# Local attention cut into 32-query pieces: six groups of 192 queries in place of ten, and strided value products in four array tiles

## The chip, the cores and the metric

The kernel runs on one core of a Trainium2 chip. The metric is device time in microseconds (us), the median of three runs of the whole program. The names of the engines are those of the profile: PE is TensorE, DVE is VectorE, ACT is ScalarE, POOL is GpSimd, SP is SyncE, whose queue issues all DMA transfers here.

## The reference

Attention over 2 sequences, 8 heads, 576 positions, 64 numbers per head; then two feed-forward parts on the 1152 tokens that come out. The change touches only the attention.

```python
rel = pos[:, None] - pos[None, :]
mask_local   = (rel >= 0) & (rel < 32)                          # heads 0 to 3
mask_strided = (rel >= 0) & (pos[None, :] % 32 == pos[:, None] % 32)   # heads 4 to 7
scores = np.where(masks, scale * q @ k.T, -1e9)
attn = softmax(scores)            # maximum taken off, sum + 1e-9 below
x = (attn @ v)                    # to [1152 tokens, 512]
h = np.maximum(x @ w_in, 0.0);  x = (h * h) @ w_out             # 512 -> 2048 -> 512
out = sum over e of p[:, e] * (np.maximum(x @ w1[e], 0.0) @ w2[e])     # 4 experts, 512 -> 1024 -> 512
```

A query of a local head sees 32 keys: its own and the 31 before it. A query of a strided head sees at most 18: the positions with its own remainder by 32.

## The kernel before

**Stages.** The tokens are three blocks of 384. The first feed-forward part takes block 0 (steps of one 128-wide slice of the 2048 hidden columns each), then block 1, then a part in which blocks are taken in pairs with fewer products, then the experts. Each large product is three matmuls of one pass (lines 788 to 790, of `mm3`; lines 1328 to 1330 for the experts), 384 or 512 columns wide. Block 0 needs the attention of the first 384 positions of sequence 0, so three strided and three local groups of that sequence come first ("startup"); the other groups are put between the steps of blocks 0 and 1 ("second", "third").

**One attention group** (`attend`). Loads of k, q and v by SP; scores on PE into a PSUM bank; a mask, either added on PE by a matmul with the identity (`ON_PE`, lines 426 and 497) or by DVE (line 554); the maximum on DVE (561); then either one exponent per unit on ACT with the sum beside it (566), or, where `whole` is set, a subtraction on DVE (571), one exponent on ACT (572) and a sum on DVE (573); reciprocal (574, 575); a product with it on POOL or DVE (576); transposes on PE (435 strided, 506 local); a copy to `pt` on ACT or DVE (545, 547); value products on PE (447 strided, 516 local); and the results as a rounded part (587, 589) and a rest (593) into `x`. The operands of scores and values are 4-byte floats; each of these matmuls stands in the trace as two records.

**Local groups.** A group is 128 queries (two groups: 64) of four heads. A unit is 64 queries of two heads (2 x 64 = 128 rows) on 64 + 32 = 96 keys. Scores: two matmuls of 64 x 64 weights and 96 columns per unit, one in rows 0 to 63 of the array with results in partitions 0 to 63, the other in rows and partitions 64 to 127. Each unit has one transpose and two value matmuls with 96 rows, 64 columns of weights and 64 columns of data. There are 18 units in a sequence.

**Strided groups.** 4 x 3, 4 x 3 or 4 x 2 remainders a group, three groups in a sequence, eight units. The value matmuls stand in two 64 x 64 parts of the array: rows 0 to 63 to partitions 0 to 63, and 64 to 127 to 64 to 127.

**Order.** `Plan.run` is a list scheduler that runs when the kernel is built. Each task has costs in ns by engine, a rank, what it comes after and the buffers that it takes; the model's order becomes the order on each engine's queue. While PE has nothing ready early on, it gives PE matmuls of no use on the tile `idle` (line 1477, `filler`), until the first product of step 0. The ranks come from constants (`FIRST` for the startup scores, `LKQ` and `LV` for their loads, `EARLY`, `LW`, `CONV`, `FETCH` for weights).

Of the kernel before, what the change touches and what calls it, by code (L numbers as in the profile page):

```python
# [33 lines left out]
CB = P + 2 * WIN + N3 + N2  # L34
NEG = -8.0e9
# [33 lines left out]
class Plan:  # L69
# [9 lines left out]
    SAME, CROSS, DMA = 100, 200, 2200  # L79
# [14 lines left out]
    def add(self, engines, emit, after=(), rank=0, take=(), free=(), adds=(), behind=None, quiet=False, tenses=(), relaxes=(), port=False):  # L94
        t = Plan.Task()
        t.engines = dict(engines)
# [7 lines left out]
    def run(self):  # L104
        import heapq

        waits, then = {}, {}
# [6 lines left out]
        events, count, done, now, fill = [], 0, 0, 0, True  # L114
# [11 lines left out]
        while done < len(self.tasks):  # L126
# [4 lines left out]
            while events and events[0][0] == now:  # L131
# [6 lines left out]
                elif what == "end":  # L138
                    t = x
                    done += 1  # L140
                    for env, key in t.free:
                        ring, tile_ = env["_" + key]
                        self.rings[ring].append(tile_)
                    for ring, tiles in t.adds:
                        self.rings[ring] += tiles
                    for y in then.get(t, ()):
                        waits[y] -= 1
                        lag = 0 if y.behind is t or t.ran == "pe" and "pe" in y.engines else self.DMA if t.ran == "dma" else self.SAME if t.ran in y.engines else self.CROSS
# [3 lines left out]
            for e in ready:  # L152
                while idle[e] and ready[e]:
                    held, got = [], None
                    while ready[e]:
# [4 lines left out]
                        if not (t.quiet and e in self.tense or (t.port or e == "pool") and now < self.shared) and all(any(self.rings[r] for r in rings) for _, _, rings in t.take):  # L160
                            got = t
                            break
# [5 lines left out]
                    for env, key, rings in got.take:  # L168
                        r = next(r for r in rings if self.rings[r])
                        tile_ = self.rings[r].pop(0)  # L170
                        env[key], env["_" + key] = tile_, (r, tile_)
# [6 lines left out]
                    got.end = now + int(got.engines[e] * slow)  # L178
                    order.append((now, len(order), got.emit, e))
# [18 lines left out]
def tile_attention_mlp_experts(ctx: ExitStack, tc: tile.TileContext, a, out):  # L198
# [25 lines left out]
    AHEAD = 10013  # L224
    END2 = 24614
    END3 = 330
    CONV = 22941
    R_LOW, R_HI = 5016, 616
    CONV1 = 31773
    CONV2 = -8455  # L230
    FETCH = 252
    WITH2 = 817
    PE_SLICE = 1914
    SQ = (0, 23, 0)
    R_MASK = -916
    ON_PE = (1, 0, 1, 0, 0, 0, 0, 0, 0, 0)
    FILL = 0
    R_MAX = -6105
    R_EXP = -6564
    R_NORM = 9634  # L240
    R_T = 1235
    R_V = 6312
    R_X = 13702
    R_LO = -53571
    R_OUT = 2681
    FIRST = (-22394, 16695, 607, 23035, 8563, 1593)
    WHOLE = (1, 1, 1, 0, 0, 0)
# [61 lines left out]
    def mm_r(n):  # L309
        return int(n / 2.4) + 13  # L310
# [1256 lines left out]
```

## Time and profile before

| what | us |
|---|---|
| median of 3 runs | 615.62 (615.57 to 615.78) |
| span of the profiled execution | 614.7 |
| PE busy in the span | 608.4 (99%) |
| DVE busy | 452.9 (74%) |
| ACT busy | 302.4 (49%) |
| POOL busy | 125.4 (20%) |
| granted TensorE clock, mean | 0.999 |

The profile gives the span of its one execution, from the first instruction to the last, and no other time of it; the runs' median is 0.92 us above that span. Shares are of the span. The times of matmuls overlap, because they are pipelined: what one of them takes from PE is read from the distance between starts, not from its duration.

### The profile page before, as it was taken

The numbers are of one execution on the slowest core, as the hardware profiler recorded it, in microseconds if no ns is written. First come the engines' busy times: TensorE is split into PE (matmuls) and PEld (weight loads), VectorE is DVE, ScalarE is ACT, GpSimd is POOL, SyncE is SP. The second block draws the span as 40 slices with busy tenths as digits, with TensorE's granted clock in tenths as the row PEclk, the third lists the DMA queues.
The fourth block names the chain that finished last, engine by engine and source line by source line (L and its number), as shares of the span: only waits on it lengthen the run. The fifth ranks groups of instructions, "written<-read, shape, count | busy, mean of one in ns | idle before, by whom it ended". The sixth has DMA issues, their size and how long they took to land.

```text
span 614.7 us, 10054 instructions
## 1 busy us (share of the span) xinstructions
PE 608.4 (99%) x3737; PEld 558.4 (91%) x3737; DVE 452.9 (74%) x900; ACT 302.4 (49%) x705; POOL 125.4 (20%) x150
## 2 busy tenths in 40 slices
PE   8999999999999999999999999999999999999997
PEld 5898999999999999998898989898998989898996
DVE  5997958774797984977666675858866776987654
ACT  3676875656464653665244534344344534344330
POOL 2421202310010101032031231312141322224000
PEclk9999999999999999999999999999999999999999
DMA  8987332131213100020110202020201203020012
GB/s 262 315 262 204 110 110 92 34 108 66 102 50 89 36 0 18 1 86 18 38 49 20 84 18 86 18 86 17 71 16 36 70 17 86 18 86 1 1 52 103
DMA packets 37441, 45.14 MB, mean 73 GB/s; under 512 B 4688, under 2 KB 26640, under 8 KB 37392
## 3 DMA queue, kind: packets, MB, share of 16 engines
q1 hardware_dynamic: 37392, 44.50, 23.7%
q8 instruction: 29, 0.48, 0.3%
q14 instruction: 20, 0.16, 0.1%
HBM read 42.13 MB, written 2.36 MB: 72 GB/s over the span
## 4 chain that ended last, share of the span: by engine, by line
PE 97%; DMA 1%; ACT 0%; DVE 0%; SPq 0%; issue 0%; POOL 0%; ACTq 0%
PE bh L788 12%; PE bh L790 12%; PE bh L789 12%; PE by L1329 11%; PE by L1328 11%; PE by L1330 11%; PE by L788 5%; PE by L790 5%; PE by L789 5%; PE ba L788 4%; PE ba L790 4%; PE ba L789 3%; PE ba L516 1%; PE ba L502 1%; DMA q<-in_ql_dram 1%; DMA k<-in_ks_dram 1%
## 5 line engine op out<-in xcount | busy, mean ns | idle before, releaser
L1281 DVE SCALAR_TENSOR_TENSOR acc<-by,pe,acc 128x512 f32<-128x512 f32 (+1 forms) x109 | 79.3, 743 | 24.2 <-PE by L1330 23.9
L788 PE MATMUL bh<-x,w 128*128 128x384 f32 x234 | 80.4, 344 | 0.0
L790 PE MATMUL bh<-x,w 128*128 128x384 f32 x234 | 78.4, 335 | 0.0
L789 PE MATMUL bh<-x,w 128*128 128x384 f32 x234 | 78.4, 335 | 0.0
L1226 POOL TENSOR_TENSOR sf<-raw,raw 128x256 f32<-128x256 f32 x40 | 32.1, 812 | 185.8 <-DMA raw<-in_w_dram 95.9
L1237 ACT ACTIVATE w<-sf 128x256 fp32r<-128x256 f32 x110 | 42.0, 406 | 35.8 <-POOL sf L1226 35.8
L1329 PE MATMUL by<-o,h 128*128 128x512 f32 (+1 forms) x134 | 52.3, 390 | 0.0
L1328 PE MATMUL by<-o,h 128*128 128x512 f32 (+1 forms) x134 | 52.0, 388 | 0.0
L788 PE MATMUL by<-h,w 128*128 128x384 f32 x152 | 51.8, 341 | 0.0
L1330 PE MATMUL by<-o,h 128*128 128x512 f32 (+1 forms) x134 | 51.7, 386 | 0.0
L790 PE MATMUL by<-h,w 128*128 128x384 f32 x152 | 50.8, 334 | 0.0
L789 PE MATMUL by<-h,w 128*128 128x384 f32 x152 | 50.8, 334 | 0.0
L788 PEld LDWEIGHTS bh<-x,w 128*128 128x128 f32 x234 | 43.9, 188 | 2.5 <-DVE r L1448 1.1
L789 PEld LDWEIGHTS bh<-x,w 128*128 128x128 f32 x234 | 44.0, 188 | 0.4
L790 PEld LDWEIGHTS bh<-x,w 128*128 128x128 f32 x234 | 43.9, 188 | 0.0
L1350 ACT ACTIVATE h<-r 128x384 fp32r<-128x384 f32 x26 | 13.7, 525 | 53.6 <-DVE r L1448 53.6
L1226 POOL TENSOR_TENSOR sf<-sf,raw 128x256 f32<-128x256 f32 x40 | 32.2, 815 | 29.1 <-DVE w L1245 29.0
L1448 DVE TENSOR_TENSOR r<-r,bh 128x384 f32<-128x384 f32 x50 | 27.6, 551 | 12.9 <-ACT r L1443 8.3
L789 PE MATMUL bh<-w,w 128*128 128x384 f32 x110 | 36.9, 336 | 0.0
L790 PE MATMUL bh<-w,w 128*128 128x384 f32 x110 | 36.9, 335 | 0.0
L788 PE MATMUL bh<-w,w 128*128 128x384 f32 x110 | 36.8, 335 | 0.0
L1258 ACT ACTIVATE o<-raw 128x512 fp32r<-128x512 f32 x30 | 18.8, 631 | 35.5 <-PE by L1330 35.1
(286 smaller groups left out, 1607.7 us busy)
## 6 DMA issues: line engine op xcount, KB each, us to landing
raw<-in_wi_dram SPq DMA_DIRECT2D x16, 512.0 KB, 3.5
raw<-in_wo_dram SPq DMA_DIRECT2D x16, 512.0 KB, 3.9
raw<-in_w_dram SPq DMA_DIRECT2D x64, 128.0 KB, 2.7
raw<-in_w_dram SPq DMA_DIRECT2D x32, 256.0 KB, 2.8
out_dram<-acc SPq DMA_DIRECT2D x8, 256.0 KB, 2.0
v<-in_vs_dram SPq DMA_DIRECT2D x6, 256.0 KB, 5.1
v<-in_vl_dram SPq DMA_DIRECT2D x8, 192.0 KB, 5.4
k<-in_kl_dram SPq DMA_DIRECT2D x8, 160.0 KB, 4.9
```

The source lines that it names most:

```text
L788: nc.tensor.matmul(dst, lhsT=wh, rhs=xh, start=start, stop=False, skip_group_check=again)
L789: nc.tensor.matmul(dst, lhsT=wh, rhs=xl, start=False, stop=False, skip_group_check=again)
L790: nc.tensor.matmul(dst, lhsT=wl, rhs=xh, start=False, stop=stop, skip_group_check=again)
L1226: nc.gpsimd.tensor_tensor(out=value(dst), in0=value(x), in1=value(y), op=ALU.subtract if n in MINUS else ALU.add)
L1237: nc.scalar.activation(out=op_slot(env["op"])[:, 0].rearrange("p k f -> p (k f)"), in_=value(src), func=AF.Copy, scale=float(sign))
L1258: nc.scalar.activation(out=late[env["w2"]][:, 0], in_=f32(raws[f]["raw"][:, DM:]), func=AF.Copy)
L1281: nc.vector.scalar_tensor_tensor(out=acc, in0=o, scalar=pcol, in1=acc, op0=ALU.mult, op1=ALU.add)
L1328: nc.tensor.matmul(o, lhsT=h[:, 0, ts], rhs=w[:, 0], start=new, stop=False)
L1329: nc.tensor.matmul(o, lhsT=h[:, 0, ts], rhs=w[:, 1], start=False, stop=False)
L1330: nc.tensor.matmul(o, lhsT=h[:, 1, ts], rhs=w[:, 0], start=False, stop=stop)
L1350: nc.scalar.activation(out=got(env["hid"])[:, 0], in_=src(), func=AF.Relu)
L1448: nc.vector.tensor_tensor(out=at_(), in0=at_(), in1=bank["bank"][:, :TB], op=ALU.add if sign > 0 else ALU.subtract)
```

## The change

Local attention: a group is 192 queries, six groups instead of ten. A unit is now 32 queries of all four heads (4 x 32 = 128 rows) on 32 + 32 = 64 keys. A score matmul has 64 x 32 weights and 64 columns, and its results go to 32 partitions, so that the four heads use two row halves and four column strips of the array. The probabilities lie in `p` with 32 zero columns in front of three units of 64, and two transposes for each 96 queries take 128 of these columns each, the second window overlapping the first. Value matmuls take 32 columns of data: for the first and third 32 queries of a chunk they take 64 rows of weights (the four quarters of the array, results in two PSUM banks), for the middle ones 96 rows. The results of a group are moved in two parts.

Strided values of sequence 1 (`four`) are laid into four quarters of the array and two banks; those of sequence 0 stay. Their v load becomes two transfers. The fp32 identity is no longer loaded: DVE makes it and the two band masks from `cb` (`set_up`). The masks of a strided group of sequence 1 move from PE to DVE, `whole` is set for all but one of the local groups after startup. The planner's delays, costs and all ranks have other values; so the order of loads and tasks differs throughout. `set_up` is ahead of all scores in the plan.

```diff
-LOCAL = [[(0, 128), (128, 128), (256, 128), (384, 128), (512, 64)], [(0, 128), (128, 64), (192, 128), (320, 128), (448, 128)]]
-WQ = 64
+NQ_LOCAL = 192
+WQ = 96
+QB = 32
 WIN = WQ + STRIDE
+KEYS = QB + STRIDE
+PLACE = (1, 0, 2)
+BAR = QB + 3 * KEYS
...
-    SAME, CROSS, DMA = 100, 200, 2200
+    SAME, CROSS, FROM_PE, TO_PE, DMA = 40, 125, 205, 260, 2200
+    FIRST_DMA = 700
+    SWITCH = 96
...
-    ON_PE = (1, 0, 1, 0, 0, 0, 0, 0, 0, 0)
+    ON_PE = (1, 0, 0, 0, 0, 0, 0)
-    FIRST = (-22394, 16695, 607, 23035, 8563, 1593)
-    WHOLE = (1, 1, 1, 0, 0, 0)
+    FIRST = (-10664, -21928, 10634, -16154, -76519)
+    WHOLE = (1, 1, 0, 0, 1, 1, 1, 1, 1, 1, 1, 0)
-    LKQ = (-8725, -8905, -8392, -8132, -7820, -7895)
-    LV = (-8661, -8282, -6737, -7657, -6434, -5679)
+    LKQ = (-9530, -55365, -19117, -7603, -3595)
+    LV = (5544, -85907, 1533, 13101, 30113)
-    L_CB = -10608
+    L_CB = -31388
...
-    t_ci = plan.add({"dma": dma(P * P * 4)}, lambda e: nc.sync.dma_start(out=ident, in_=a["ci"]), rank=L_ID)
+    def set_up(e):
+        nc.vector.tensor_copy(ident, cb[:, :P])
+        c = COLS["local"][0]
+        for x in range(P // QB):
+            rows, o = slice(x * QB, (x + 1) * QB), c + x % (WQ // QB) * QB
+            nc.vector.tensor_copy(bands["local"][rows], cb[rows, o : o + KEYS])
+        nc.vector.tensor_copy(bands["first"], bands["local"])
+        nc.vector.memset(bands["first"][:, :STRIDE], NEG)
+
+    t_ci = plan.add({"dve": 1300}, set_up, after=[t_cb], rank=L_ID)
...
     class Strided:
...
-                nc.sync.dma_start(out=env["v"], in_=a["vs"][b, self.j])
+                src = a["vs"][b, self.j]
+                if not self.four:
+                    nc.sync.dma_start(out=env["v"][:, : U * D], in_=src)
+                    return
+                src = src.rearrange("(t p) (k c) -> k p t c", t=2, k=2)
+                for k in range(2):
+                    nc.sync.dma_start(out=env["v"][k * D : (k + 1) * D, : U * D].rearrange("p (t c) -> p t c", t=2), in_=src[k])
...
         def values(self, env):
             n = self.n
-            for h in range(2):
-                for g in range(GROUPS):
-                    c, q = (h * GROUPS + g) * n, g * P + h * D
-                    for k in range(2):
-                        rows = slice(k * D, k * D + n)
-                        nc.tensor.matmul(env["X"][k * D : (k + 1) * D, c : c + n], lhsT=env["v3"][rows, 2 * g + h, :], rhs=env["pt"][rows, q : q + n], start=True, stop=True)
+            for x in range(2):
+                for h in range(2):
+                    for y in range(2):
+                        for k in range(2):
+                            t, g = (y, x) if self.four else (k, 2 * x + y)
+                            c = (h * 2 + x) * n if self.four else (h * GROUPS + g) * n
+                            rows, q = slice(k * D, k * D + n), (t * 2 + g if self.four else g) * P + h * D
+                            v = env["v3"][rows, t, g, h] if self.four else env["v3"][rows, x, y, h]
+                            nc.tensor.matmul(env["X", k if self.four else 0][t * D : (t + 1) * D, c : c + n], lhsT=v, rhs=env["pt"][rows, q : q + n], start=True, stop=True)
...
     class Local:
         def masks(self):
-            first = 2 if self.t0 == 0 else 0
-            return [x for x in (("first", 0, first), ("local", first, self.units)) if x[1] < x[2]]
+            return [("local", 0, 1), ("first", 1, 2), ("local", 2, 3), ("local", 3, 6)] if self.t0 == 0 else [("local", 0, self.units)]
...
             for u in range(units):
-                j, t = divmod(u, 2)
-                for h in range(2):
-                    hd = slice(h * D, (h + 1) * D)
-                    nc.tensor.matmul(s[hd, u * WIN : (u + 1) * WIN], lhsT=env["q3"][hd, u, :], rhs=env["k3"][hd, t, j * WQ : j * WQ + WIN], start=not masked, stop=not masked or u == units - 1)
+                j, x = divmod(u, WQ // QB)
+                for t in range(2):
+                    for h in range(2):
+                        hd, r, c = slice(h * D, (h + 1) * D), (2 * h + t) * QB, (3 * j + PLACE[x]) * KEYS
+                        nc.tensor.matmul(s[r : r + QB, c : c + KEYS], lhsT=env["q3"][hd, j, t, x * QB : (x + 1) * QB], rhs=env["k3"][hd, t, u * QB : u * QB + KEYS], start=not masked, stop=not masked or u == units - 1)

         def transposes(self, env):
-            for u in range(self.units):
-                nc.tensor.transpose(env["T"][:WIN, u * P : (u + 1) * P], env["p"][:, u * WIN : (u + 1) * WIN], ident)
+            p, k = env["p"], self.chunks
+            for j in range(k):
+                nc.tensor.transpose(env["T"][:, j * P : (j + 1) * P], p[:, j * BAR + WQ : (j + 1) * BAR], ident)
+            for j in range(k):
+                nc.tensor.transpose(env["T"][:, (k + j) * P : (k + j + 1) * P], p[:, j * BAR : j * BAR + P], ident)

         def values(self, env):
-            for u in range(self.units):
-                for h in range(2):
-                    j, t = divmod(u, 2)
-                    c = t * self.nq + j * WQ
-                    nc.tensor.matmul(env["X"][h * D : (h + 1) * D, c : c + WQ], lhsT=env["v3"][:, 4 * j + 2 * t + h, :], rhs=env["pt"][:WIN, u * P + h * WQ : u * P + (h + 1) * WQ], start=True, stop=True)
+            pt, v = env["pt"], env["v3"]
+            for j in range(self.chunks):
+                for t in range(2):
+                    for h in range(2):
+                        for k in range(2):
+                            rows, q = slice(k * KEYS, (k + 1) * KEYS), j * P + (2 * h + t) * QB
+                            c = (t * self.chunks + j) * QB * (2 - k)
+                            nc.tensor.matmul(env["X", k][h * D : (h + 1) * D, c : c + QB], lhsT=v[rows, j, 2 * t + h], rhs=pt[rows, q : q + QB], start=True, stop=True)
+            for j in range(self.chunks):
+                for t in range(2):
+                    for h in range(2):
+                        q, c = (self.chunks + j) * P + (2 * h + t) * QB, (t * self.chunks + j) * QB * 2 + QB
+                        nc.tensor.matmul(env["X", 0][h * D : (h + 1) * D, c : c + QB], lhsT=v[:WQ, j, 2 * t + h], rhs=pt[:WQ, q : q + QB], start=True, stop=True)
...
-        t = plan.add({"pe": g.cost_s - (0 if masked else mm_r(n))}, lambda e: g.scores(env, masked), after=[t_cb, t_go, *loads[:2], *(transposed[-3:-2] if len(rings) == 1 else [])], ...
+        t = plan.add({"pe": g.cost_s + (mm_r(n) if masked else 0)}, lambda e: g.scores(env, masked), after=[t_cb, t_ci, t_go, *loads[:2], *(transposed[-3:-2] if len(rings) == 1 else [])], ...
...
-    startup = [Strided(0, j) for j in range(3)] + [Local(0, j) for j in range(3)]
+    startup = [Strided(0, j, False) for j in range(3)] + [Local(0, j) for j in range(2)]
-    second = [Local(0, 3), Local(0, 4)] + [Strided(1, j) for j in range(3)] + [Local(1, 0), Local(1, 1)]
+    second = [Local(0, 2)] + [Strided(1, j) for j in range(3)] + [Local(1, 0)]
-    third = [Local(1, j) for j in (2, 3, 4)]
+    third = [Local(1, j) for j in (1, 2)]
```

## Rows read from the trace of the kernel before

**Rows 1.** The page: busy time of PE, and the chain by engine.

```profile
PE 608.4 (99%) x3737; PEld 558.4 (91%) x3737; DVE 452.9 (74%) x900; ACT 302.4 (49%) x705; POOL 125.4 (20%) x150
...
PE 97%; DMA 1%; ACT 0%; DVE 0%; SPq 0%; issue 0%; POOL 0%; ACTq 0%
```

**Rows 2.** Windows: span and busy time of each engine, granted clock, DMA share.

```profile
30.00:40.00 10.00, 10.00 (x160) 9.05 (x154) 9.80 (x27) 7.44 (x20) 2.80 (x4) 1.00 0.99 308
40.00:50.00 10.00, 9.90 (x131) 8.86 (x125) 9.53 (x28) 7.02 (x16) 1.83 (x2) 1.00 0.55 164
```

**Rows 3.** Timeline of PE: start, duration, line, in one run of local values.

```profile
55.93 0.34 PE L790 MATMUL by<-h,w 128*128 128x384 f32 x1
56.20 0.69 PE L516 MATMUL ba<-pt,v 96*64 96x64 f32 x16
...
57.09 0.34 PE L789 MATMUL by<-h,w 128*128 128x384 f32 x1
...
58.72 0.33 PE L788 MATMUL bh<-x,w 128*128 128x384 f32 x1
...
59.07 0.34 PE L790 MATMUL bh<-x,w 128*128 128x384 f32 x1
59.34 0.45 PE L516 MATMUL ba<-pt,v 96*64 96x64 f32 x8
...
60.00 0.34 PE L789 MATMUL bh<-x,w 128*128 128x384 f32 x1
```

**Rows 4.** Timeline of PE: strided values with local scores behind them.

```profile
45.95 0.34 PE L790 MATMUL by<-h,w 128*128 128x384 f32 x1
46.22 1.14 PE L447 MATMUL ba<-pt,v 54*64 54x54 f32 x32
47.19 0.84 PE L502 MATMUL ba<-k,q 64*64 64x96 f32 x16
...
48.24 0.34 PE L789 MATMUL by<-h,w 128*128 128x384 f32 x1
```

**Rows 5.** Timeline of PE: strided scores of 54 and 36 columns, strided values of 36.

```profile
33.46 1.01 PE L430 MATMUL ba<-k,q 64*54 64x54 f32 x32
...
39.44 0.75 PE L430 MATMUL ba<-k,q 64*36 64x36 f32 x32
...
50.46 1.12 PE L447 MATMUL ba<-pt,v 36*64 36x36 f32 x32
```

**Rows 6.** Timeline of PE: four transposes between two large products.

```profile
54.42 0.34 PE L790 MATMUL bh<-x,w 128*128 128x384 f32 x1
54.59 0.60 PE L506 MATMUL ba<-ident,p 128*96 128x128 f32 x4
...
55.21 0.34 PE L789 MATMUL by<-h,w 128*128 128x384 f32 x1
```

**Rows 7.** Groups by form: weights, data, count, busy us, mean ns.

```profile
L1477 PE MATMUL by<-idle 128*128 128x512 bf16 x23 | 7.7, 479 | 1.0 <-DVE idle L1481 1.0
L502 PE MATMUL ba<-k,q 64*64 64x96 f32 x128 | 7.0, 248 | 0.5 <-DMA q<-in_ql_dram 0.4 <-DVE p L554 0.2
```

**Rows 8.** Timeline of PE at the start: first fillers, first scores, first large product.

```profile
0.98 4.02 PE L1477 MATMUL by<-idle 128*128 128x512 bf16 x9 [0.98 <-DVE idle L1481]
4.80 0.57 PE L426 MATMUL ba<-cb 128*128 128x432 bf16 x1
...
21.75 0.52 PE L788 MATMUL bh<-x,w 128*128 128x384 f32 x1
```

**Rows 9.** Timelines of SP and DVE at the start: load of `cb`, loads behind, DVE's first task.

```profile
0.74 0.39 SPq L365 DMA_DIRECT2D cb<-in_cb_dram  x1
...
2.12 0.43 SPq L413 DMA_DIRECT2D k<-in_ks_dram  x1
...
6.67 0.61 DVE L561 TENSOR_REDUCE st<-ba 128x8 f32<-128x432 f32 x1 [5.74 <-PE ba L430]
```

**Rows 10.** A piece of the chain: one mask on PE.

```profile
29.55 0.29 PE ba L426
```

More of the change, by code (lines that the diff above doesn't have):

```diff
@@ L92, in ring, with add @@
         self.rings[name] = list(tiles)
-    def add(self, engines, emit, after=(), rank=0, take=(), free=(), adds=(), behind=None, quiet=False, tenses=(), relaxes=(), port=False):
+    def add(self, engines, emit, after=(), rank=0, take=(), free=(), adds=(), behind=None, quiet=False, tenses=(), relaxes=(), port=False, tiled=False):
         t = Plan.Task()
+        t.tiled = tiled
         t.engines = dict(engines)
@@ L105, in run, with room @@
         import heapq
-        waits, then = {}, {}
+        waits, then, tiled = {}, {}, False
+        def room(take):
+            claimed = {}
+            for _, _, rings in take:
+                r = next((r for r in rings if len(self.rings[r]) > claimed.get(r, 0)), None)
+                if r is None:
+                    return False
+                claimed[r] = claimed.get(r, 0) + 1
+            return True
         for t in self.tasks:
@@ L159, in run @@
                             continue
-                        if not (t.quiet and e in self.tense or (t.port or e == "pool") and now < self.shared) and all(any(self.rings[r] for r in rings) for _, _, rings in t.take):
+                        if not (t.quiet and e in self.tense or (t.port or e == "pool") and now < self.shared) and room(t.take):
                             got = t
@@ L277, in tile_attention_mlp_experts @@
     cb = const.tile([P, CB], BF16, name="cb")
+    bands = {k: const.tile([P, KEYS], BF16, name=k) for k in ("local", "first")}
     idle = const.tile([P, P], BF16, name="idle")
@@ L309, in mm_r @@
     def mm_r(n):
-        return int(n / 2.4) + 13
+        return 229 if n == 512 else int(n / 2.4) + 13
     def act(n):
@@ L429, in scores @@
                     hd = slice(h * D, (h + 1) * D)
-                    nc.tensor.matmul(s[h * D : h * D + n, u * n : (u + 1) * n], lhsT=env["q3"][hd, u, :], rhs=env["k3"][hd, u, :], start=not masked, stop=not masked or u == U - 1)
+                    g, t = divmod(u, 2)
+                    c = (t * GROUPS + g % 2 * 2 + g // 2 if self.four else u) * n
+                    nc.tensor.matmul(s[h * D : h * D + n, c : c + n], lhsT=env["q3"][hd, u, :], rhs=env["k3"][hd, u, :], start=not masked, stop=not masked or u == U - 1)
         def transposes(self, env):
@@ new lines, in results, with ends @@
+        def results(self):
+            blk, c = divmod(self.b * S + self.t0, TB)
+            parts = []
+            for k in range(2):
+                n = 2 - k
+                def ends(env, k=k, n=n):
+                    dst = xt[blk][:, :, 0:2, c : c + self.nq].rearrange("p s t (j q) -> p s t j q", q=WQ)[:, :, :, :, 2 * k * QB : (2 * k + n) * QB]
+                    return dst, env["X", k][:, : 2 * self.chunks * n * QB].rearrange("p (t j q) -> p t j q", t=2, q=n * QB)
+                parts.append((blk, 2 * self.chunks * n * QB, k, ends))
+            return parts
```

244 lines of the change are left out of this document (138 added, 106 removed).

## The prediction

> **What bounds the kernel now.** I read the chain of waits first: 97% of what ended last is PE [rows 1], and PE is busy for 608.4 of the 614.7 us span. The reader is to see there that no other engine holds the end: after the first 22 us the time is the sum of what stands in PE's queue. The windows come next, since PE could be only just ahead of another engine: in the stretch where attention and the first steps overlap, DVE is busy for 19.33 of 20 us while PE loses 0.1 [rows 2]. So an edit is worth what it takes out of PE's queue, as long as DVE does not fall behind between 30 and 50 us. Last I read the timeline of PE at the start. Nine fillers run before the first scores at 4.80, and the first large product starts at 21.75 [rows 8]; there are 23 fillers in all [rows 7], so 14 lie between. A filler of 512 columns is some 0.23 us (384 columns are 0.175, from 58.72 to 59.07 for two [rows 3]), so about 3.2 us of this stretch is PE time without use.
>
> **What a record costs PE.** Durations overlap, so I take distances between starts of the large products around a run and subtract their own two strides, 0.35. A run of 16 local value records moves the next product by 57.09 - 55.93 - 0.35 = 0.81, a run of 8 by 60.00 - 59.07 - 0.35 = 0.58 [rows 3]. That is 0.23 for eight records, 28.8 ns each, and 0.35 for the run as such. Strided values with local scores behind them take 48.24 - 45.95 - 0.35 = 1.94 [rows 4]; less 0.35, and less 32 x 28.8 = 0.92 for the values, 16 score records take 0.67, 42 ns each. Transposes have no cost of the run: 55.21 - 54.42 - 0.35 = 0.44 for four, 0.11 each [rows 6].
>
> The transposes have the array to themselves: 110 ns for 128 columns, 0.86 ns a column. By that a lone score record of 96 columns would take 82 ns and a lone value record of 64 some 55. They take 42 and 28.8. So two records run side by side, and a part of the array has a pace of its own: 84 ns at 96 columns, 57.6 at 64. Strided scores agree: 1.01 against 0.75 for 32 records of 54 and of 36 columns [rows 5] is 0.45 ns a column, or 0.90 within a part. One more thing is to be seen there: strided values take 1.12 with 36 columns of data, and 1.14 with 54 [rows 4, 5]. Both have 64 columns of weights, so for them it is the weights that set the pace, and shorter data saves nothing.
>
> **The change, part by part.** No row shows four parts of the array at work. If each keeps its pace of 57.6 ns, a record in four parts costs 57.6 / 4 = 14.4 ns. The upper bound is 28.8, the price of two parts. I take 14.4, since the pace of a part held for three kinds of records; the quickest record so far is 0.45 x 36 = 16.2 ns [rows 5], which is nearer to 14.4 than to 28.8.
>
> Local scores: 144 records (128 and 16 [rows 7]; the code gives 36 units x 2 matmuls x 2 records) at 42 ns are 6.05 us. Afterwards 6 groups x 24 matmuls x 2 are 288 records of 64 columns: 288 x 14.4 = 4.15. That is -1.90.
> Local values: 144 x 28.8 = 4.15. Afterwards 6 x 32 records in four parts and 6 x 16 with 96 rows, which can only stand in two: 192 x 14.4 + 96 x 28.8 = 5.53. That is +1.38: 32 columns of data cost what 64 did.
> Transposes: 24 for 36, -12 x 0.11 = -1.32.
> Strided values of sequence 1: 96 records from 28.8 to 14.4, -1.38.
> Masks on PE: that of one strided group goes, -0.29 [rows 10]; one local mask fewer, but the first one in four pieces, 0.
> Cost of the runs: 12 runs of local scores and values for 20, at 0.35 each. But runs stand together (one 0.35 for both in rows 4), and each local value run changes from 64 rows to 96 inside. I take 0; the ends are -1.4 (half of eight) and +1.0 (six inner changes at half a run's price).
> Sum: -1.90 + 1.38 - 1.32 - 1.38 - 0.29 = -3.5 us.
>
> The Trainium skill has a rule against such small pieces: "TensorEngine Tiling (Array Packing)", section Performance Considerations, says that every matmul carries about 60 cycles of overhead, and that no tiling factor is to be taken from a dimension that is already small. Taken as a price that parts can't share, this is an estimate of 25 ns a record at 2.4 GHz, and the sum would be +2.2 us. The slope in rows 5, which leads to 16.2 ns a record, speaks against that reading; the equal times of 36 and 54 columns speak for the rule's advice.
>
> **Start.** `cb` goes from the first load to the fourth. That is the place of the load issued at 2.12 instead of 0.74 [rows 9], so 1.4 us later, with three loads ahead of it in the queues. `set_up`, seven small DVE instructions, then stands in the plan between `cb` and the first scores; from nothing, if something else is later, to some 1.4 us (an estimate, 0.2 each against 0.61 for 432 columns [rows 9]). DVE is idle till 6.67 and pays nothing; what waits are the scores, and behind them the whole chain of softmax. I take 2.1 us for the first scores, out of 0 to 2.8. Against it stand the 3.2 us of later fillers, which can shrink: two local groups instead of three are in the startup, the same 384 columns of softmax each, so a third of that work leaves DVE, and the weights of step 0 are asked for earlier. I take 0 in all; the ends are -3 and +2.5.
>
> **DVE between 25 and 60.** Added: the mask of a strided group (0.6), subtraction and sum for two local groups (4 x 0.55), and a third strided result split into more pieces (0.6 in all). Gone: a third of the local columns and their small column work, an estimate of 1.9 from the same 0.6 a pass. Net +1.5 where 0.7 of 20 us is free [rows 2]. I cost it at nothing because PE's queue holds steps that do not need these groups; without that cover it costs up to 1.5, and block 1's first product is late next. Loads and weight splits are reordered throughout. Transfers hold 1% of the chain before [rows 1]; I take 0.
>
> Span 614.7 - 3.5 = 611.2. The median lies 0.9 above the profiled span, so the forecast is 612.1.
>
> **The rivals.**
> A shorter start: the planner's other delays and ranks remove most of the fillers, -2 to -4 more, 608 to 610. For it: 3.2 us of fillers. Against it: the first scores come later.
> A longer start, or DVE as the bound: the late `cb` and the whole softmax cost 2.5 to 4 together, 614.6 to 616. For it: 19.33 of 20. Against it: DVE loses a third of the local columns.
> Weights in single file: the 28.8 ns of a record with 64 weight columns could be one path for the whole array and not a part's own pace. Then 288 records (192 local, 96 strided) stay at 28.8, +4.15, so +0.6 in all: 616.2. The equal times in rows 4 and 5 fit this as well. The skill's 60 cycles, above, are a rule of this kind; they would give 617.8.
> The other side, two parts at a time: all 576 records at 28.8 are +8.3, so +4.8 in all: 620.4. It decides from 20.5 ns a record on (14.4 + 3.5/576), in the local scores and values. For it: no row shows more than two parts at work. Against it: pairs across rows (scores) and across columns of the same rows (96-row values) both run side by side.
> Loads moved in the later stages leave a product without weights: 617 and more. Nothing in the rows speaks for it.
>
> **How the numbers follow.** Forecast 0.52, with its own range of 610.3 to 614.0 (16.2 ns would give 613.1, the runs' cost -1.4 to +1.0). Shorter start 0.12. Longer start or DVE 0.18. Single file 0.08. Two at a time 0.05. Late loads 0.05. The range 608.5 to 616.5 leaves out half of the shorter start, half of the single file and most of the last two, about 0.19. A measurement of this kernel can tell about 0.2% from no change, that is 614.4 to 616.85. Faster: the forecast, the shorter start and a third of the longer one, 0.70. No change: 0.09 of the longer start, 0.04 of the single file, 0.02 of the others, 0.15. Slower: the rest, 0.15.
>
> **What would show it.** In the timeline of PE: 48 local score records in about 0.7 us plus a run's 0.35, 48 value records in some 0.92 plus 0.35 to 0.5, 32 strided value records of sequence 1 in 0.46 plus 0.35. At 28.8 these would be 1.4, 1.4 and 0.92. First scores near 7, first large product within 1.5 of 21.75. PE waits after 25 us of no more than 0.5. The prediction is wrong if the first large product moves by over 2 us, if PE waits for DVE between 30 and 60, or if the records do not run four side by side.

## The result, and the profile after

The changed kernel takes 621.52 us (median of 4 runs, 621.10 to 622.30) where the kernel before takes 615.70: a ratio of 1.0095, 95% interval 1.0081 to 1.0109. It is slower by 5.8 us; I had forecast 3.5 less, and the time lies 5 us above the upper end of the range. The profiled execution has a span of 619.3 us against 614.7. That is 4.7 more and not 5.8, since the profiled execution of the kernel before was a long one: in its other executions a time of 615.6 goes with a span of 613.8, 1.8 less, and so it is in the kernel after (621.10 and 619.3).

The page of the kernel after, busy times and the chain by engine, answers to [rows 1]:

```profile
PE 609.3 (98%) x4026; PEld 556.5 (90%) x4026; DVE 458.7 (74%) x893; ACT 301.5 (49%) x688; POOL 122.7 (20%) x148
...
PE 88%; DVE 6%; DMA 3%; issue 1%; ACT 1%; SPq 1%; DVEq 0%
```

PE is still the bound, but 12% of the chain lies elsewhere now, where 3% did. The windows from 30 us on answer to [rows 2] (columns as there):

```profile
30.00:40.00 10.00, 9.62 (x123) 8.56 (x122) 8.50 (x19) 7.39 (x16) 5.22 (x5) 1.00 1.03 303
40.00:50.00 10.00, 10.00 (x183) 9.00 (x182) 9.18 (x27) 5.89 (x15) 3.24 (x3) 1.00 0.76 232
50.00:60.00 10.00, 8.64 (x83) 7.91 (x81) 9.53 (x24) 6.43 (x15) 4.02 (x4) 1.00 0.41 149
```

PE loses 1.4 us between 50 and 60 us. From 30 to 50 us GpSimd is busy for 8.46 us, where it was 4.63. PE's waits in the whole span (line, what it waited for: us, times, longest):

```profile
PE bh L883 <- DVE h L961: 1.0, 1, 1.0
PE ba L484 <- DMA q<-in_qs_dram: 0.9, 1, 0.9
PE ba L489 <- DVE x L688: 0.8, 1, 0.8
PE by L564 <- issue: 0.8, 1, 0.8
PE bh L883 <- DVE r L1543: 0.7, 1, 0.7
PE ba L501 <- ACT pt L634: 0.6, 1, 0.6
PE ba L581 <- issue: 0.4, 1, 0.4
PE ba L581 <- ACT pt L634: 0.3, 1, 0.3
```

In the kernel before, PE waits for 1.5 us in all behind its first filler, the last time at 62.7 us.

PE's timeline at the start answers to [rows 8] (L478 masks, L564 local scores, L489 transposes, L1572 fillers, L501 strided values):

```profile
0.99 5.16 PE L1572 MATMUL by<-idle 128*128 128x512 bf16 x15 [0.99 <-DVE idle L1576]
5.98 0.35 PE L478 MATMUL ba<-cb 128*128 128x432 bf16 x1
...
15.45 0.30 PE L564 MATMUL by<-k,q 64*32 64x64 f32 x4 [0.78 <-issue]
15.69 0.66 PE L489 MATMUL ba<-ident,p 128*128 128x128 f32 x4
16.18 0.60 PE L489 MATMUL by<-ident,p 128*128 128x128 f32 x4
16.62 2.54 PE L1572 MATMUL by<-idle 128*128 128x512 bf16 x11
19.08 1.14 PE L501 MATMUL ba<-pt,v 54*64 54x54 f32 x32
...
28.10 0.45 PE L883 MATMUL bh<-x,w 128*128 128x384 f32 x1
```

First scores 1.2 us later, first large product 6.4 us later; but much of the first groups' attention then lies ahead of that product and not behind it. So I count by products: after 300 large products (the attention is done in both) the kernel after is 0.97 us behind, after 550 by 2.23, after 2000 by 2.83, after 2100 by 4.03, at the last by 4.85. Up to the 300th, the distances from start to start on PE sum up like this: fillers 6.67 before and 9.65 after, attention 34.63 and 31.66, large products 56.32 and 57.27, waits included. Attention gives 3.0 us, the fillers take 3.0. Of the waits, 1.4 us before and 2.1 after stand in attention's sum (without them it gives 3.6), and 1.6 after in that of the large products (0.8 for `x`, 0.6 and 0.3 for `pt`, all between 36 and 58 us).

The forecast of the records can be read in three runs of attention between large products:

```profile
42.65 0.34 PE L885 MATMUL by<-h,w 128*128 128x384 f32 x1
42.92 0.69 PE L501 MATMUL ba<-pt,v 54*64 54x54 f32 x32
...
43.82 0.34 PE L884 MATMUL by<-h,w 128*128 128x384 f32 x1
...
60.42 0.34 PE L885 MATMUL bh<-x,w 128*128 128x384 f32 x1
60.69 1.54 PE L564 MATMUL ba<-k,q 64*32 64x64 f32 x96
...
62.45 0.34 PE L884 MATMUL by<-h,w 128*128 128x384 f32 x1
...
68.11 0.34 PE L885 MATMUL bh<-x,w 128*128 128x384 f32 x1
68.38 0.83 PE L581 MATMUL ba<-pt,v 64*64 64x32 f32 x32
69.14 0.66 PE L586 MATMUL ba<-pt,v 96*64 96x32 f32 x16
...
70.01 0.34 PE L884 MATMUL bh<-x,w 128*128 128x384 f32 x1
```

By the method of [rows 3, 4], from the last large product ahead of a run to the second one behind it, 32 strided values take 43.82 - 42.65 - 0.35 = 0.82 (forecast 0.81), 96 local scores 62.45 - 60.42 - 0.35 = 1.68 (1.73), and 48 local values 70.01 - 68.11 - 0.35 = 1.55, of which 0.16 is a pause within the run; the next two such runs, at 73.97 and 77.47 us, take 1.39 (1.27 to 1.42). With the run's 0.35 taken off, a score record costs 1.33 / 96 = 13.9 ns and a strided value 0.47 / 32 = 14.7. The single starts within the runs say the same: score records in four parts start every 14.0 ns, value records every 14.6, with 54, 36 or 32 columns of data, and the values with 96 rows, which stand in two parts, every 29.1. Four parts do run side by side, at the forecast's 14.4.

### The profile page after: what moved, and what is told of

It is laid out like the page before. It is cut to its first block, busy times and chain, and to the rows that moved or that the text cites. A ratio compares the mean times of both kernels' runs of the same rounds, so it can differ in the third digit from the quotient of the medians.

```text
span 619.3 us, 10613 instructions
## 1 busy us (share of the span) xinstructions
PE 609.3 (98%) x4026; PEld 556.5 (90%) x4026; DVE 458.7 (74%) x893; ACT 301.5 (49%) x688; POOL 122.7 (20%) x148
## 4 chain that ended last, share of the span: by engine, by line
PE 88%; DVE 6%; DMA 3%; issue 1%; ACT 1%; SPq 1%; DVEq 0%
PE bh L883 11%; PE bh L885 10%; PE bh L884 10%; PE by L1424 10%; PE by L1425 10%; PE by L1423 10%; PE by L883 4%; PE by L885 4%; PE by L884 4%; PE ba L885 3%; PE ba L883 3%; PE ba L884 3%; DVE acc L1376 1%; DMA raw<-in_wo_dram 1%; DMA pe<-in_pe_dram 1%
## 5 line engine op out<-in xcount | busy, mean ns | idle before, releaser
L859 POOL TENSOR_TENSOR w<-val,w 128x512 fp32r<-128x512 f32 x18 | 23.8, 1325 | 118.2 <-ACT w L853 103.3
L1356 DVE TENSOR_TENSOR o<-raw,o 128x512 fp32r<-128x512 f32 x30 | 21.4, 716 | 21.8 <-ACT o L1353 21.7
```

Of the source, the lines that this page charges most:

```text
L859: eng[e].tensor_tensor(out=w[:, 1, cs], in0=value(), in1=f32(w[:, 0, cs]), op=ALU.subtract)
L1356: nc.vector.tensor_tensor(out=late[env["w2"]][:, 1], in0=f32(raws[f]["raw"][:, DM:]), in1=f32(late[env["w2"]][:, 0]), op=ALU.subtract)
```

## The experiments

Ratios are against the kernel before on the same chip, with 95% intervals; the kernel before took 615.9 to 616.4 there, and 615.70 beside the kernel after. Between runs of different sets the ratios are compared, not the times.

**The wide products.** The experts have 855 products of 512 columns. For 801 of them the data come from tiles `o`, which hold weights of the network, and the array's weights from `h`, `t` or `x`; these stand 233.1 ns apart in stretches of 27, before 229.3. (The other 54 have their data in a tile `w` and take 227 ns in both kernels.) Their operations are the same. What differs is where their tiles lie: `o` keeps its place at the right end of SBUF, and the bigger `cb` and the two bands move `h`, `t` and `x` on the left by 384 bytes. The offset of `h` from `o`, modulo 512 bytes, goes from 448 to 320. An unused tile behind `pe_s` changes nothing but this:

```
     pe_s = const.tile([P, NT // P], F32, name="pe_s")
+    const.tile([P, 32], F32, name="pad")     # 128 bytes; 16, 48, 96 elsewhere
```

> The changed kernel with an unused 128-byte tile behind pe_s: everything on the left side of SBUF moves up by 128 bytes, the w2 tiles o on the right stay. Nothing else differs. Theory A (distance): the 512-column expert products take 232.7 ns from start to start after the change and 229.2 before it, because the tiles that hold their weights (h, x, t) lie at another distance from the moving data o, modulo 512 bytes: 448 before, 320 after. With 128 bytes more it is 448 again: pace back to 229.2, the time 3.0 us below the changed kernel, 618.5. Rival B (traffic): the pace comes from the changed order of work on the other engines; then the pad changes nothing, 621.5.

> The same with 192 bytes: the distance becomes 0 modulo 512, which is that of the few expert products whose weights and data both lie on the left (w with h or t, 227 ns in both traces). Theory A: 227 to 228 ns for all 855 of them, 4 to 5 us below the changed kernel, about 617. Rival B: 621.5, no change.

> The kernel before with an unused 384-byte tile behind pe_s, so that its left side lies where that of the changed kernel lies; no other difference. Theory A: 512-column pace 232.7 instead of 229.2, 3 us slower than before, 618.7. Rival B: 615.7, no change.

> The kernel before with an unused 64-byte tile behind pe_s: distance 0 modulo 512. Theory A: pace 227 to 228 instead of 229.2, 1 to 2 us faster than before, 614. Rival B: 615.7, no change.

| kernel | offset mod 512 | ns a product | median us | ratio |
|---|---|---|---|---|
| before | 448 | 229.3 | 616.35 | |
| after | 320 | 233.1 | 621.52 | 1.0095 [1.0081, 1.0109] |
| after_pad128 | 448 | 229.3 | 618.41 | 1.0031 [1.0020, 1.0041] |
| after_pad192 | 0 | 228.2 | 618.07 | 1.0024 [1.0008, 1.0040] |
| before_pad384 | 320 | 233.1 | 618.73 | 1.0037 [1.0024, 1.0050] |
| before_pad64 | 0 | 228.2 | 615.43 | 0.9987 [0.9977, 0.9996] |

Timelines of before, of after and of after_pad128, the first and the last of the same 27 products:

```profile
590.19 0.39 PE L1328 MATMUL by<-o,h 128*128 128x512 f32 x1
...
596.15 0.39 PE L1330 MATMUL by<-o,x 128*128 128x512 f32 x1
```

```profile
594.84 0.39 PE L1423 MATMUL by<-o,h 128*128 128x512 f32 x1
...
600.90 0.39 PE L1425 MATMUL by<-o,x 128*128 128x512 f32 x1
```

```profile
591.29 0.39 PE L1424 MATMUL by<-o,h 128*128 128x512 f32 x1
...
597.26 0.39 PE L1426 MATMUL by<-o,x 128*128 128x512 f32 x1
```

5.96, 6.06 and 5.97 us for 26 strides. Over all 855 it is 198.97 us in after, 195.93 in before and in after_pad128. The pace goes with the offset in both kernels and in both directions: 3.0 us of the loss in the trace, shown; by the ratios it is 3.9 (after) and 2.3 (before). A little of it comes back: behind the 550th large product, the products of 384 columns with both operands in tiles `w` take 75.95 us at the offset 320 and 76.29 at 448, in both kernels. The 0.3 us between after_pad128 and after_pad192 is not clear of noise, and 618.07 misses the 617 of the expectation, though the pace is the one forecast. All that follows is built on after_pad128 or after_pad192, but for two runs on the kernel before.

**VectorE and GpSimd.** Timelines of after, VectorE, GpSimd and PE, where the wait for `h` arises:

```profile
137.32 2.38 DVE L788 TENSOR_TENSOR w<-sf,w 128x512 fp32r<-128x512 f32 x2
139.62 0.55 DVE L961 TENSOR_TENSOR h<-bh,h 128x384 fp32r<-128x384 f32 x1
...
137.73 1.42 POOL L859 TENSOR_TENSOR w<-val,w 128x512 fp32r<-128x512 f32 x1 [40.30 <-ACT w L853]
...
140.22 0.44 PE L883 MATMUL bh<-x,w 128*128 128x384 f32 x1 [0.97 <-DVE h L961]
```

One of the two passes of L788 takes its usual 0.68, the other 1.78: it stands still while GpSimd's pass runs. The Trainium skill, "SBUF — State Buffer", section Who interferes with whom, says that an operation of VectorE with two inputs in SBUF contends with one of GpSimd that reads SBUF, over ports that one of them holds alone; the trace agrees, 1.10 us. By 100 us, ten operations of VectorE are longer than the median of their form by over 0.4 us, 7.4 us in all, and each of them overlaps one of GpSimd; before it is three, 1.6 us. GpSimd has 14 of the weight passes by then where it had 4.

```
-            emit(e)
+            if e == "pool":
+                pools += 1
+                e = "dve" if pools == 25 else e     # the pass at 137 us
+            emit(e)
```

> The kernel after with 128 unused bytes, in the same order, but one of GpSimd's weight passes (the one at 137.2 us, beside which VectorE's pass took 1.79 instead of 0.69 us) is issued on VectorE, behind the last part of the hidden tile h. Theory A, the two engines hold each other up when they work at the same time: no pass on VectorE takes over 0.75 us there, TensorE's wait for h near 139 us (0.98) goes, the 550th large product starts at 142.6 to 142.9 instead of 143.6, and the time falls by 0.7 to 1.0 us against after_pad128 (618.4 us, 2.1 above before). Theory B, VectorE is simply late there: the pass costs it 0.7 us more, the wait stays or grows, and the time is 618.4 or more.

617.74 us, 1.0022 [1.0013, 1.0030]. VectorE's timeline:

```profile
137.12 1.28 DVE L794 TENSOR_TENSOR w<-sf,w 128x512 fp32r<-128x512 f32 x2
138.32 0.55 DVE L967 TENSOR_TENSOR h<-bh,h 128x384 fp32r<-128x384 f32 x1
138.79 0.68 DVE L865 TENSOR_TENSOR w<-val,w 128x512 fp32r<-128x512 f32 x1
```

The two passes take 1.28, the wait is gone, the 550th product comes 0.74 earlier: theory A in the trace. The gain in the time, 1.0031 to 1.0022, is not clear of noise. In its trace 0.9 us go again at 435 us, where PE waits for `r`; the kernel after has that wait (0.7) as well, and there too two operations of VectorE, at 425.8 and 426.7 us, take 0.97 and 0.95 instead of 0.42 beside two of GpSimd. It is no fixed price of the change: of the 14 traces of the kernel after and its variants nine have it and five have not, after_pad128 and after_pad192 among these. What decides is open.

pad128_norm gives VectorE six normalisations in the same way (`pools` 8, 12, 13, 15, 18, 19).

> The kernel after with 128 unused bytes, in the same order, but the six normalisations of the later units that GpSimd does between 38 and 72 us are issued on VectorE (0.5 to 0.6 us each, 3.5 us in all). Theory A, what GpSimd does there stretches VectorE's operations beside it by 0.5 to 0.8 us each: VectorE gains about as much as it takes on, the exponents are ready earlier, and the 300th large product starts at 98.3 to 99.0 us (99.0 in after_pad128), the time within 0.7 us below 618.4. Theory B, VectorE is the bound of that stretch and the overlap costs little: the 300th product comes 1 to 3 us later and the time is 619.4 to 621.4.

618.97 us, 1.0056 [1.0036, 1.0075]; 300 products are done at 99.29 instead of 99.02 us, and PE's wait for `x` grows from 0.8 to 1.4. VectorE takes on 3.5 us of work and PE loses a few tenths: nearer to A in the trace, no gain in the time. Of the two places tried, the collision cost PE time at 137 us, where it was about to wait for VectorE.

**The start.** The first maximum is at 9.28 us, 6.67 before [rows 9]; VectorE has the first weight conversion ahead of it (its timeline in after):

```profile
8.20 0.43 DVE L840 TENSOR_SCALAR mid<-mid 128x512 uint32<-128x512 uint32 x1 [1.08 <-ACT mid L834]
8.66 0.69 DVE L845 SCALAR_TENSOR_TENSOR val<-raw,mid 128x512 uint32<-128x512 uint32 x1
9.28 0.96 DVE L657 TENSOR_REDUCE st<-ba 128x8 f32<-128x432 f32 x2
```

ScalarE has more to do as well: `WHOLE` takes the third strided group from one exponent to eight, from 11.26 to 13.5 us. Windows of before and of after (columns as in [rows 2]; ScalarE 2.60 and 4.09 of 5 us):

```profile
10.00:15.00 5.00, 4.62 (x46) 2.96 (x45) 4.56 (x17) 2.60 (x9) 1.93 (x2) 1.00 1.01 296
```

```profile
10.00:15.00 5.00, 4.67 (x130) 2.94 (x125) 4.78 (x15) 4.09 (x23) 0.78 (x1) 1.00 1.04 384
```

No run changes this entry alone; pad128_oldranks, below, puts it back together with the whole old order.

pad128_lw0 ranks that load later (`LW`, -25050 to 0), and the planner makes a new order of everything.

> The kernel after with 128 unused bytes, and the load of the first half of the first weights ranked later, so that VectorE takes the first strided maxima and subtractions ahead of the weight conversion. Theory A, the late start comes from the conversion standing ahead of the first softmax in VectorE's queue: the first maximum starts at 7.2 to 7.5 us instead of 9.3, the first values 1.5 to 2 us earlier, and the time falls by 1 to 2 us to 616.4 to 617.4. Theory B, VectorE's sum of work up to the first large product is what counts: the conversion is only late instead, the first large product starts at 28 us or later, and the time is 618.4 or more.

621.05 us, 1.0082 [1.0064, 1.0101]; first large product at 31.69 us. That fits theory B, but the new order is changed throughout, so it does not show it.

pad128_drop keeps the order and leaves fillers out, which compute nothing that is used:

```
-                order.append((now, len(order), self.filler[2], "pe"))
+                nf += 1
+                order.append((now, len(order), self.filler[2] if nf not in self.DROP else (lambda e: None), "pe"))
```

> The kernel after, with 128 unused bytes behind pe_s (the run after_pad128: 618.4 us, first strided values at 18.9, first large product at 28.2), and with the order of all its work kept, but the last 20 of the 36 filler products (those from about 10.7 us on, 11 of them between the transposes and the first values) are not issued. Theory A, the fillers are pure delay: ScalarE's copies of the transposed exponents are done at about 17.4, so the first values start there, the first large product at 26.7 to 27.2, and the time falls by 1.0 to 1.5 us to about 617.1. Theory B, something else would end the same wait (a load of v, the copies, instruction fetch): PE shows waits of the same sum in the place of the fillers, the first large product stays within 0.4 us of 28.2 and the time within 0.6 us of 618.4. Theory C, the granted clock falls without the fillers: the scores and values after the gap take up to twice as long and the time rises by 1 us or more.

It left out 24 and not 20. 618.87 us, 1.0058 [1.0041, 1.0074]. In the trace the first values start at 17.42, the first large product at 26.80, and the gain of 1.4 us (1.5 after 300 products) holds up to the 2000th product. The chain to the first values now runs over ScalarE, 1.79 us of exponents and 1.12 of copies. The gain is not seen in the time: the four runs spread from 616.88 to 620.65, and the two longest have a mean clock of 0.992 and 0.991. A holds for the delay and C for the clock.

pad128_start leaves out fillers 17 to 36 and puts the conversion behind the first maxima; pad128_drop11 leaves out the last 11 and has pad128_hdve's edit.

> The kernel after with 128 unused bytes, fillers 17 to 36 not issued, and on VectorE the first weight conversion (with what ScalarE and GpSimd do behind it) moved behind the first two maxima, the first subtraction and the first negation; all else in its order. Theory A, the first softmax is late because the conversion stands ahead of it: its first maximum starts at 7.2 to 7.5 us instead of 9.4, the first strided values at 16 to 16.6 instead of 17.4 (pad128_drop), the first large product at 25.5 to 26.3, and the time is 1 to 2 us below after_pad128 (2.1 above before). Theory B, the sum of VectorE's and ScalarE's work up to the first values sets the start: the maximum starts early, but the first values and the first large product stay within 0.5 us of pad128_drop (17.4 and 26.8), and the time is 2 to 3 us above before.

> The kernel after with 128 unused bytes, only the last 11 of the 36 fillers not issued (those between the transposes and the first values), and GpSimd's pass at 137 us on VectorE as in pad128_hdve (617.7 us, 1.5 above before). Theory A, those 11 are 2.5 us of delay for 1.4 us of waiting: 1.0 us less than pad128_hdve in the trace from the first large product on, and in the time, 0.5 above before. Theory B, what is gained at the start is waited for behind it, since VectorE sets the pace up to 60 us or the granted clock falls in some runs, as in pad128_drop: within 0.4 us of pad128_hdve or above it.

pad128_start: 621.99 us, 1.0091 [1.0077, 1.0105], mean clock 0.985 to 0.992 in all five runs, so the time tells little. The trace does: the first maximum starts at 7.38, but the second, which stands ahead of the first subtraction, waits to 9.61 for scores whose `q` is late (PE waits 1.2 us for it), and the first values start at 17.85, within the 0.5 us of theory B: in this trace the conversion had filled a gap. The rest of the trace says little, since the clock is at its lower level from about there (0.50 from 20 to 30 us) and the first large product comes at 31.92. pad128_drop11: 616.86 us, 1.0015 [0.9995, 1.0036], and here the clock parts the runs: six with 0.999 or 1.000 take 614.46 to 616.40 us, six with 0.988 to 0.994 take 617.31 to 621.06. Its windows (columns as in [rows 2]):

```profile
15.00:20.00 5.00, 3.56 (x60) 2.93 (x62) 4.80 (x15) 4.39 (x16) 0.83 (x1) 0.97 1.00 361
20.00:25.00 5.00, 5.00 (x81) 4.47 (x79) 3.80 (x13) 2.14 (x6) 0.00 (x0) 0.50 0.88 289
25.00:30.00 5.00, 5.00 (x115) 4.07 (x114) 2.49 (x8) 2.60 (x5) 2.32 (x2) 0.51 0.91 279
```

PE has waited before (0.72 and 0.53 us, 3.56 of 5 us busy), then the clock is at its lower level, 1.2 GHz, for some ten us. The waits alone do not decide it: the trace of pad128_drop waits longer there (PE busy for 2.90 of 5 us) and keeps 1.00. So the fillers are delay and, in a part of the runs, what holds the clock. pad192_keep5 and pad192_keep3 keep 5 and 3 of the 11, with the offset 0 and the edit of pad128_hdve.

> The kernel after with 192 unused bytes (wide products at 228.2 ns), GpSimd's pass at 137 us on VectorE, and 5 of the 11 fillers between the transposes and the first values kept. In pad128_drop11, which kept none, the runs with a mean clock of 0.999 to 1.000 took 614.5 to 616.4 us and those with 0.988 to 0.994 took 617.3 to 621.1. Theory A, those fillers cost more than the wait that they cover, but some are needed to hold the clock: with 5 the clock stays at 0.999 or 1.000 in all runs, the first values come 0.9 to 1.2 us earlier against the 11, and with 0.8 us from the pace the time is 614.5 to 615.6, 0.5 to 1.6 below before. Theory B, the clock falls in some runs with 5 as well: the runs spread over 614 to 621 and the median is not below before.

> As pad192_keep5, with 3 of the 11 fillers kept, which end just before ScalarE's second copy of the transposed exponents does. Theory A: a wait of 0.2 to 0.5 us in the place of two fillers, no fall of the clock, 614.3 to 615.6 us. Theory B: the clock falls (mean 0.988 to 0.994) in a part of the runs, between the half of them in pad128_drop11 and none, and the median lies at 615 to 617.

With 5: 617.03 us, 1.0024 [1.0007, 1.0040]; five of the twelve runs have a mean clock of 0.994 to 0.997 and take 617.3 to 620.8. With 3: 615.44 us, 0.9992 [0.9980, 1.0004]; one run of twelve at 0.994. Its windows and PE's timeline:

```profile
15.00:20.00 5.00, 3.61 (x51) 2.69 (x51) 4.06 (x12) 3.77 (x14) 0.83 (x1) 1.00 0.94 338
20.00:25.00 5.00, 5.00 (x133) 4.25 (x136) 5.00 (x17) 4.00 (x10) 0.00 (x0) 1.00 0.93 294
```

```profile
16.88 0.81 PE L1581 MATMUL by<-idle 128*128 128x512 bf16 x3
17.62 1.14 PE L510 MATMUL ba<-pt,v 54*64 54x54 f32 x32
```

By the ratios this is 6 us faster than the kernel after, three to four of them from the offset, and level with the one before. The clock fell in five of twelve runs with 5 fillers, in one of twelve with 3, in six of twelve with none: too few runs to tell 3 from 5, and why fewer fillers should hold it better is not explained.

**Parts of the change.** pad128_two has the strided values of sequence 1 in two tiles (`Strided(1, j, False)`); pad128_each has three more local groups with their exponents one by one on ScalarE (`WHOLE`; the "nine local units" of its expectation are nine groups, four of them local); pad128_oldranks has the ranks and lead times of before.

> The kernel after with 128 unused bytes, and the strided values of the second sequence two at a time again, as before (three units of 32 products, 1.07 to 1.12 us instead of 0.60 to 0.69 for each). Theory A, TensorE is the bound where they stand: the time rises by 1.2 to 1.4 us to 619.7. Theory B, VectorE sets the pace of that stretch (28 to 76 us) and TensorE has slack there: the time stays within 0.4 us of 618.4.

> The kernel after with 128 unused bytes, and three of the nine local units whose maximum is subtracted in one operation of VectorE have it as the bias of six exponents on ScalarE. Theory A, VectorE bounds the stretch from 50 to 60 us (9.53 of 10 us busy there): the wait for x near 57 us (0.8) goes, and the time falls by 0.5 to 1.0 us to about 617.6. Theory B, ScalarE's six short exponents for a unit take longer than the one operation saves: waits for pt grow, and the time is 618.4 to 619.5.

> The kernel after with 128 unused bytes, its operations and the lags of its planner, but the ranks and lead times of before (where lists are shorter, their first entries). Theory A, the new operations are cheap and it is the new order that costs: the start is as in before (first large product at 21 to 24 us) and the time within 1 us of before or below it. Theory B, the operations bring the late start with them (nine larger units in place of ten, two of them ahead of the first large product, on a VectorE that is busy throughout): 619 us or more, with the first large product at 26 us or later or with waits of TensorE of over 4 us up to 100 us.

620.35 us, 1.0076 [1.0054, 1.0098]; 620.90, 1.0081 [1.0066, 1.0096]; 620.21, 1.0071 [1.0054, 1.0089]. Undoing the four tiles costs more than the 1.4 us of A, but neither the order nor the clock stays: the planner makes a new order, and two of the four runs have a mean clock of 0.997 and 0.995. The price of the tiles alone can't be read from it. Exponents one by one make PE wait 2.5 us in one place, for VectorE's `x` and not for `pt` as in theory B; the time lies above B's range, with a mean clock of 0.996 or 0.997 in all four runs (0.94 and 0.89 from 40 to 60 us in the trace). With the old ranks the first large product is at 27.26 and fillers take 11.13 us: theory B, so the late start is not the new ranks' doing alone.

before_four does the reverse: the kernel before with the strided values of sequence 1 in four tiles; before_four64 adds 64 bytes.

> The kernel before, with the strided values of the second sequence in four tiles (their loads, the order of their columns and their results in two banks go with it) and nothing else; all of its work up to the first of these units keeps its order. Theory A, my term for this edit: three units of 32 products at 0.62 instead of 1.08 us, so 1.4 us less, 614.5 to 615.0 where before takes 616. Theory B, VectorE's second write of x for each block, and the new order that the planner makes of it, give it back: within 0.5 us of 616. Theory C, the two banks that a unit now takes hold up the scores behind it: 617 us or more.

> The kernel before_four with 64 unused bytes behind pe_s. If the pace of the wide products follows the distance of the tiles alone, as in before_pad64 (228.2 instead of 229.2 ns, 0.8 us over 855 products), and adds to what the four tiles give: 613.5 to 614.3 us. If they overlap or the four tiles give nothing: 615.2 to 616.

617.10 us, 1.0013 [1.0004, 1.0021], and 616.70, 1.0008 [0.9999, 1.0016]. The 96 values take 1.84 us from start to start, where the same 96 in two tiles take 3.00 in the kernel before: 1.2 us less. PE's waits show where this went:

```profile
PE bh L820 <- DVE h L898: 1.3, 2, 0.8
PE ba L466 <- ACT pt L577: 1.0, 1, 1.0
```

The values now wait for the copies of the exponents, and large products for `h`. Up to the 300th product attention takes 35.87 us, 1.2 more than before. The saving on PE is real and is given back within 60 us, by 100 us. That is theory B's mechanism, but the 0.9 us above before are more than its 0.5. They reach the 617 of theory C, whose cause is hardly there: PE waits once, for 0.2 us, for a bank to be emptied (by VectorE's `x`).

## Why the prediction was wrong

**What a record costs PE** was right, in its mechanism and in its size. Records in four parts start every 14.0 to 14.6 ns where I took 14.4, and the three runs above take what was forecast to within 0.12 us, the pause aside. So single file and two parts at a time fall, and with them the estimate of 25 ns a record by the Trainium skill's 60 cycles ("TensorEngine Tiling (Array Packing)", section Performance Considerations): the trace does not agree, 14.0. (My +2.2 for it also took 25 ns for the records with 96 rows; at their 28.8 it is +2.6.) The sum of the terms was -3.5; attention's distances gave -3.0, and -3.6 without its waits.

**Start** is the step that failed: "I take 0 in all; the ends are -3 and +2.5." The fillers went from 6.67 to 9.65 us, +3.0, outside even the upper end: 1.2 of it ahead of the first scores, 1.8 behind them, where 21 fillers stand instead of 14. The first scores came within my bounds (1.2 late; I took 2.1, bounds 0 to 2.8), but I hoped that the later fillers would shrink with the smaller softmax, and counted VectorE's work without ScalarE's. In the trace they stand for a chain that got longer: a subtraction that waits for the second unit's `q`, transposes behind scores that stall, copies behind ScalarE's exponents. Nor can they just be taken out: without them the trace gains 1.4 of the 3.0 us, and the granted clock falls in part of the runs. How much of the 3 us the new operations force stays open; keep3's trace wins back about one of after_pad128's. By the prediction's own signs it was wrong here (the first large product moved by 6.4 us, not 2) and in the next step (PE waits for DVE between 30 and 60).

**DVE between 25 and 60**, costed at nothing with an end of 1.5: PE waits 0.8 for `x` there and another 0.8 for `pt`, ScalarE's copies, 1.6 in all. What I had not seen is GpSimd: it lengthens VectorE's operations. PE pays 1.0 us for that near 140, which pad128_hdve shows, and in nine of 14 traces about as much near 435, where the cause is argued and not shown; both lie far behind the changed work.

**Loads**, costed at nothing, are 3% of the chain; among PE's waits only those for `q` at the start are theirs, 0.9 us after and 1.0 before. But no step looked at the experts, since the change does not touch them: their 3.0 us come from an address. This item is as large as the start's, and no rival held it.

In the trace: -3.0 attention with its waits, +3.0 fillers, +0.95 large products up to the 300th (with the waits for `x` and `pt`), +1.3 by the 550th (the wait for `h`), +1.0 at 437 us for `r` (from start to start), +3.0 pace, are +6.25; the last product is 4.85 late. The other 1.4 are small gains behind the 550th: six pairs of products on `x` in the kernel before, from 331 to 571 us, each 0.14 us longer than in the kernel after (0.9), the products with both operands in `w` (0.3), and the rest in steps of under 30 ns. The prediction had no term for these.

## What to carry to other kernels

A tile that grows moves all behind it: compare the stride of untouched products first, and try a few dozen bytes of padding before you judge an edit. Where PE is the bound by a hair, time taken out of its queue counts only if what feeds it (copies, softmax, the other engine at VectorE's side) comes earlier too. Fillers that hold the clock are part of the schedule: shorten them, and look at the clock of every run.

## What the runs showed of the hardware

- A product of 512 columns takes 228.2, 229.3 or 233.1 ns with the offset of its two operands in SBUF at 0, 448 or 320 bytes modulo 512, in two kernels each. No other offsets were tried.
- Four-byte value and score records in four parts of the array start every 14.6 and 14.0 ns; values in two parts every 29.1. The values have 64 columns of weights; whether they have 54, 36 or 32 columns of data makes no difference.
- PE stalls for 0.3 to 1.3 us amid such runs with nothing to wait for in the profile (at 15.45 and 27.26 us in after, in ten of the 14 traces of it and its variants, in none of the five of the kernel before and its variants). Instruction fetches of 16 KB start at 13.03 and 24.83 us, with the DMA share near 1.0; that they are the cause was not tried, and the kernel before has such fetches (at 11.02 and 22.05 us) without the stall.
- An operation of VectorE on 128x512 that took 0.68 us alone took 1.78 beside one of GpSimd of 1.42, and 1.28 for two when GpSimd's was moved.
